# Splitting one exponential in two halves and moving the score rows of 48 turns of an attention kernel

## The chip, the cores and the metric

The kernel runs on one core of one Trainium2 chip. The metric is the device time of one execution in microseconds (us), as a median of runs. Profiles are of one execution each. In the text PE is the matrix engine (its weight loads are listed apart as PEld), ACT the scalar engine, DVE the vector engine, POOL the GpSimd engine, SP the engine that issues most DMAs. SBUF is the on-chip memory that all engines read, PSUM the eight banks into which PE writes its products; a bank holds 512 fp32 numbers in each of 128 partitions.

## The reference, cut to what matters

```python
S, D, H, F = 2048, 512, 32, 1792          # Dh = D // H = 16
xn = layernorm(x)
q, k, v = split(xn @ wqkv)                # 32 heads of 16
p = softmax(einsum("bhqd,bhkd->bhqk", q, k) * Dh ** -0.5)
s = einsum("bhqk,bhkd->bhqd", p, v).reshape(1, S, D) @ wo
h = relu(xn @ w1 + b1) ** 2
g = silu(h @ w2 + b2)
out = x + s * g
```

## The kernel before, in words

A first part normalizes x and makes q, k and v. Then comes a long loop of 64 **turns** (L1142), and a short end. The attention is cut into 1024 steps: 8 groups of four heads, 4 chunks of 512 queries, 16 blocks of 128 keys. A step has two **score pairs** p = 0 and 1, each of two heads hp = 0 and 1. A score (L511) is one multiply of a 64-row half of PE into one bank: 128 keys by 512 queries. The two scores of a pair use the two row halves of PE and run beside each other. The exponential of a score goes into an SBUF tile (ptile) that the values multiply (L863) reads later.

Turn n, with i = 8n, computes the scores of steps i+1 to i+8 and at its end multiplies the values of steps i to i+7. There are 16 score pairs in a turn. Between them PE runs the feed-forward products (gate branch, from layer 1 and 2 blocks) in the same 64-row halves. The order of a turn is written out by hand as a string of **rows**, one letter a row; in a row the two halves of PE run one multiply each, of 512 columns:

- S: both scores of a pair, into one of two **places** of two banks each (tag S, two buffers in turn). ACT takes the exponential of both banks as one 128x1024 operation (L519) into the ptile. That frees the place for the second S row after it.
- L: two products of the feed-forward part (L563), into two banks of a tile called spare (in the profile S<-xh,wf1h and the like; S<-QA,KA is a score).
- 0, 1, a, b, B: **set-aside** scores (L533). The score of one head (or, for B, of both) goes into one of the two set-aside banks, sides[0] (in the profile acc) and sides[1] (lin); DVE copies it at once to the ptile in SBUF (L538), and ACT takes the exponential there, in place, at the end of the turn. 0 is head 0 into acc with an L product in the other half, 1 head 1 into lin, a head 0 into lin, b head 1 into acc.
- / : the swap (L584). POOL writes one note (L588) as soon as the L products so far have ended, and the first L product behind the swap waits for that note, since the two halves of PE change banks.

An ordinary turn has 40 rows. Counted from 0, its S rows are rows 0, 3, 8, 12, 16, 19, 23, 27, 31, 37 and 39, the swap stands between rows 18 and 19, and the set-aside rows are 4 (B), 11 (0), 14 (1), 20 (B), 26 (0), 29 (1), 34 (0) and 36 (1). Nine of the pairs go straight to ACT (pairs 0 to 8), pairs 9 to 13 are set aside, and the last two, both of step i+8, are scored in rows 37 and 39; their exponentials are issued behind those of the set-aside pairs (L1181, L1185), because their ptile is that of step i and comes free only when the values multiply of step i has run. After the rows PE runs the values multiply of eight steps into acc, DVE takes that sum out of acc (L889 or L892), and the next turn begins: a one-element ACT copy and DVE operation (L1129, L1130) first, then row 0.

Row 0 and row 3 of the next turn use the places of the last two pairs, and its row 4 uses acc and lin again.

Of the kernel before, what the change touches and what calls it, by code (L numbers as in the profile page):

```python
# [27 lines left out]
AF = mybir.ActivationFunctionType  # L28
# [7 lines left out]
SCALE = DH ** -0.5  # L36
# [40 lines left out]
def fast_path(tc, sb, banks, env):  # L77
# [7 lines left out]
    dve, act, pool, sp = nc.vector, nc.scalar, nc.gpsimd, nc.sync  # L85
# [6 lines left out]
    def t(shape, dt, tag):  # L92

        cnt[0] += 1
        if tag in BUFS:
            turn[tag] = turn.get(tag, -1) + 1
            n = turn[tag] % BUFS[tag]
            p, tag = ps.get(tag), f"{tag}{places[n] if tag == 'S' else n}"
        else:
            p = None  # L100
        return (p or ps.get(tag, sb)).tile(shape, dt, tag=tag, name=f"{tag}_{cnt[0]}")
# [407 lines left out]
    ptile = {}  # L509

    def score(i, p, hp, dst):  # L511
        qd, qc, kb = steps[i]
        k, q = ka[qd, kb // 8], qa[qd, qc]
        r = slice(64 * hp, 64 * hp + 64)
        mm(dst, k[r, p, 128 * (kb % 8):128 * (kb % 8) + 128], q[r, p], start=True, stop=True)  # L515

    def exps(i, p, src):
        if src is not None:
            act.activation(ptile[i, p], src, AF.Exp, scale=SCALE)  # L519

    def place(i, p):
        ptile[i, p] = t([128, 2, 512], FT, f"P{2 * ((i - 1) % 8) + p}")

    def scores(i, p):

        if i < len(steps):
            sc = t([128, 2, 512], FT, "S")
            place(i, p)
            for hp in range(2):
                score(i, p, hp, sc[:, hp])  # L530
            return sc

    def aside(i, p, hp, bank):  # L533

        if (i, p) not in ptile:
            place(i, p)
        score(i, p, hp, sides[bank])
        dve.tensor_copy(ptile[i, p][:, hp], sides[bank])  # L538
# [37 lines left out]
    def lin(*halves):  # L576
        done = False
        if pair[0]:
            for half in halves:
                j = half ^ swapped[0]  # L580
                done |= pair[0][j].issue(half, lin_banks[j])
        return done

    def swap():  # L584
        if pair[0]:
            while lin(0, 1):
                pass
            f = pool.memset(note[:, notes[0]:notes[0] + 1], 0.0)  # L588
            notes[0] += 1
            for block in pair[0]:  # L590
                tc.add_manual_dep(f.ins, block.last, SYNC, reason="the products so far")
            swapped[0], fence[0] = 1, f.ins.name

    def end_pair():
        if pair[0]:
            while lin(0, 1):
                pass
            swapped[0], last, pair[0] = 0, pair[0], None
            last[0].evict()
# [46 lines left out]
    def second(c, g, i):  # L646
        ms = [m for m in range(len(PAIRS)) if PAIRS[m][0] == g]
        h, w = [hid[m] for m in ms], [wf[2, m] for m in ms]

        def evict():  # L650
            if g == 0:
                y[c, i] = t([128, 2, 512], FT, f"y{i}")
            old = b2b.unsqueeze(1).broadcast_to([128, 2, 512]) if g == 0 else y[c, i]
            dve.tensor_tensor(y[c, i], spare, old, op=OP.add)
            if g == 3:
                complete.add((c, i))

        return [Block(lambda p, k, j=j: h[k // 2][p][:, k % 2, 128 * j:128 * j + 128],
                      lambda p, k: w[k // 2][p][:, k % 2], range(2 * len(ms)), evict)
                for j in (2 * i, 2 * i + 1)]  # L660
# [9 lines left out]
    for c in ORDER:  # L670
        for m in range(len(PAIRS)):
            fill.append([lambda m=m: first(m)])
            if m in (1, 2, 4, 6):
                makes = [lambda c=c, g=m // 2, i=i: second(c, g, i) for i in range(2)]
# [164 lines left out]
    def early():  # L839
        open_banks(below, "ps2", "left", (("S0", 1024), ("S1", 1024)))  # L840
        for q in range(2):
            exps(0, q, scores(0, q))
# [28 lines left out]
    def values_of(steps_now):  # L871
        for i in steps_now:
            values(i, i == steps_now[0], i == steps_now[-1])

    def finish_early():
        early[0] = t([128, 512], FT, "ou")
        dve.tensor_copy(early[0], sides[0])
# [114 lines left out]
    def make_last():  # L992
        u = pend.pop((2, 3))
        h, l = onorm[2, 3] = on_tiles(2, 3)
        o = t([128, 512], FT, "T")
        for a in (h, o):
            pool.tensor_tensor(a, u[:, 0], u[:, 1], op=OP.mult)
        pool.tensor_tensor(l, o, h.bitcast(FT), op=OP.subtract)
# [40 lines left out]
    middle = {}  # L1039
    TURNS, LAST = len(steps) // 8, 8 * (NQ - 1)  # L1040
# [8 lines left out]
    for j, c in enumerate(ORDER):  # L1049
        for i in range(2):  # L1050
            n = per * (j + 1) + i - 1 if j < 3 else LAST + 2 + i
# [41 lines left out]
    def happen(time):  # L1093
        for fn, a in events.pop(int(2 * time), ()):
            fn(*a)
# [6 lines left out]
    sides = [t([128, 512], FT, "acc"), t([128, 512], FT, "lin")]  # L1102
    xs[0] = xT[3]

    def rest(i, dst):

        group(dst, lambda p: onorm[2, 3][p][:, cut[i]], lambda p: wos[0][p][1][:, 1])
# [18 lines left out]
    def see(i):  # L1126

        last = ptile[i, 1][:1, 1, 511:]
        act.copy(seen[:, :1], last)  # L1129
        dve.tensor_tensor(seen[:, 8:9], last, sides[1][:1, :1], op=OP.max)  # L1130
# [1 line left out]

    ASIDES = {"0": ((0, 0),), "1": ((1, 1),), "a": ((0, 1),), "b": ((1, 0),), "B": ((0, 0), (1, 1))}
    ORDINARY = "SLLSBLLLSLL0SL1LSLL/SBLLSLL0SL1LSLL0L1SLS"
    TWO_PAIRS = "SLLSbLaLLS/0SaLLLbS1LSEVSLLSLLLLBS/LLLL0LS1S"

    SHORT = "SLLSBLLLS0S1LL0S1/S0LL1SL0SL1L0LSS1"

    FIRST = "SLLSLLBLSLL0SL1LSLL/SBLLSLL0SL1LSLL0L1SLS"
    for n in range(TURNS):  # L1142
        i = 8 * n
        happen(n)
        makes = fill[n][:]
        pair[0] = makes.pop(0)()
        if n:
            see(i - 1)
        pairs = [(k, p) for k in range(i + 1, i + 9) for p in range(2)]
        short = n in (LAST, LAST + 1)  # L1150
        nd = 8 if short else 9
        direct, asides = pairs[:nd] + pairs[14:], pairs[nd:14]
        later, aside_at = [], [0, 0]
        for row in TWO_PAIRS if makes else SHORT if short else ORDINARY if n else FIRST:
            if row == "S":
                k, p = direct.pop(0)
                sc = scores(k, p)
                if k == i + 8:
                    later.append((k, p, sc))
                else:  # L1160
                    exps(k, p, sc)
            elif row == "L":
                lin(0, 1)
            elif row in ASIDES:
                for hp, bank in ASIDES[row]:
                    aside(*asides[aside_at[hp]], hp, bank)
                    aside_at[hp] += 1
                if len(ASIDES[row]) == 1:
                    lin(1 - hp)
            elif row == "/":  # L1170
                swap()
                if n == TURNS - 1:
                    make_last()
            elif row == "E":
                end_pair()
                pair[0] = makes.pop(0)()
            else:
                values_of(range(i, i + 2))
                finish_early()
        for j, (k, p) in enumerate(asides):  # L1180
            exps(k, p, ptile[k, p])  # L1181
            if j == 0:
                for fn, a in middle.pop(n, ()):
                    fn(*a)
        for a in later:  # L1185
            exps(*a)
        if n == TURNS - 1:
            two = t([128, 2, 512], FT, "S")
            for m in range(2):
                rest(m, two[:, m])  # L1190
            rest(3, sides[1])
        pieces_now = pieces_of[n] if n < len(pieces_of) else 0
        ahead = pieces_now > 0 and n % per in (0, 1, 3, 6, 7, 10, 11)
        while lin(0, 1):
            pass
        if ahead:
            split_piece()
        end_pair()
        if n == LAST + 4:
            gsb.update({(1, i): y[1, i] for i in range(2)})  # L1200
        if n == TURNS - 1:
            for m in range(2):
                end_rest(m, two[:, m])
            end_rest(3, sides[1])
        happen(n + 0.5)
        for _ in range(pieces_now - ahead):
            split_piece()
        values_of(range(i + 2 if early[0] else i, i + 8))
        finish(n)
# [27 lines left out]
    for n in range(2):  # L1237
        for i in range(2):
            for j in range(4):
                k = 8 * n + 4 * i + j  # L1240
# [137 lines left out]
```

## Time and profile before

| what | us |
|---|---|
| median of 3 runs (1207.81 to 1208.74) | 1208.66 |
| the profiled execution's own time | 1208.63 |
| its span, first to last instruction | 1206.9 |
| stretch ahead of the turns' first values multiply | 0 to 145.8 |
| stretch of the turns' values multiplies | 145.8 to 1192.8 |
| the end | 1192.8 to 1206.9 |
| DVE busy in the span | 844.3 |
| ACT busy in the span | 1042.2 |
| POOL busy in the span | 357.1 |

The span is 1.7 us shorter than the profiled execution's time. The trace's granted clock of PE is 0.999 over the span. A line of the timeline has the start in us from the span's start, the duration, the engine, the line of the kernel, the operation, the tiles written and read, shapes and the count, and in brackets how long the engine sat idle before and what ended that. Where operations of one kind overlap, they are merged in one line with a count, and the duration is that of the whole. A PEld line is the load of the weights for a multiply that comes later. Ends of multiplies are modelled, so starts are what is compared.

### The profile page before, as it was taken

To read this page: it belongs to the slowest core of one execution; us is meant where nothing else is said; L and a number is where in the kernel's file an instruction comes from. 1 tells how busy PE (TensorE), PEld (TensorE's weight loads), DVE (VectorE), ACT (ScalarE), POOL (GpSimd) and SP (SyncE) were. 2 spreads that over 40 slices of the span, in tenths; PEclk is the share of its full clock that TensorE was granted. 3 is DMA by queue.
4 is the path that set the end of the run, shared out by engine and by line. 5 is a ranking of instruction groups with operands and counts; after the bars stand their busy time and mean duration, and the time that the engine had idled before them with its cause. 6 is when DMAs were issued, how large, how long until landed. Compare 5 with 4: busy or idle time off the path is not lost.

```text
span 1206.9 us, 24222 instructions
## 1 busy us (share of the span) xinstructions
PE 1197.8 (99%) x9867; PEld 712.8 (59%) x9867; DVE 844.3 (70%) x1362; ACT 1042.2 (86%) x1232; POOL 357.1 (30%) x276
## 2 busy tenths in 40 slices
PE   9999999999999999999999999999999999999997
PEld 7888655555655555655555555555555555555554
DVE  7666767575867776757677666667775758777766
ACT  6655689889989889988999899889898889999984
POOL 6756523040312321304032122220230403322224
PEclk9999999999999999999999999999999999999999
DMA  7798914131343222224423133151422233455434
GB/s 291 297 377 312 339 56 137 45 111 44 97 155 108 72 72 84 68 77 150 119 76 102 58 93 90 45 168 45 132 80 80 78 100 80 132 189 171 159 110 141
DMA packets 107640, 155.17 MB, mean 129 GB/s; under 512 B 43386, under 2 KB 57736, under 8 KB 107524
## 3 DMA queue, kind: packets, MB, share of 16 engines
q1 hardware_dynamic: 104596, 144.60, 37.1%
q0 software_dynamic: 2352, 7.93, 2.1%
q8 instruction: 78, 1.28, 0.5%
q10 hardware_dynamic: 576, 1.05, 0.2%
q14 instruction: 38, 0.31, 0.1%
HBM read 103.87 MB, written 49.67 MB: 127 GB/s over the span
## 4 chain that ended last, share of the span: by engine, by line
PE 98%; DVE 1%; DMA 0%; issue 0%; ACT 0%; DVEq 0%
PE acc L866 37%; PE S L563 29%; PE S L515 15%; PE B L326 5%; PE acc L515 5%; PE B L127 4%; PE lin L515 2%; PE D L326 1%; PE D L253 1%; PE S L1017 0%; PE lin L326 0%; PE acc L326 0%; DMA P<-in_A_x_dram 0%; DVE P L1262 0%; DVE P L1263 0%; PE S L326 0%
## 5 line engine op out<-in xcount | busy, mean ns | idle before, releaser
L519 ACT ACTIVATE P<-S 128x1024 f32<-128x1024 f32 x702 | 662.7, 1039 | 91.8 <-PE S L515 89.0
L866 PE MATMUL acc<-P,V 128*32 128x512 f32 x4096 | 453.5, 594 | 0.0
L538 DVE COPY P<-acc 128x512 f32<-128x512 f32 x322 | 222.8, 692 | 141.5 <-PE acc L515 70.0
L519 ACT ACTIVATE P<-P 128x1024 f32<-128x1024 f32 x322 | 315.0, 1090 | 0.0
L515 PE MATMUL S<-QA,KA 64*128 64x512 f32 x1404 | 295.4, 404 | 0.0
L866 PEld LDWEIGHTS acc<-P,V 128*32 128x32 f32 x4096 | 126.2, 110 | 286.2 <-issue 265.0
L538 DVE COPY P<-lin 128x512 f32<-128x512 f32 x322 | 220.7, 685 | 1.8 <-PE lin L515 0.6
L515 PEld LDWEIGHTS S<-QA,KA 64*128 64x128 f32 x1404 | 136.4, 184 | 109.3 <-issue 41.8
L515 PE MATMUL lin<-QA,KA 64*128 64x512 f32 x322 | 126.4, 393 | 0.0
L515 PE MATMUL acc<-QA,KA 64*128 64x512 f32 x322 | 126.4, 393 | 0.0
L120 POOL TENSOR_TENSOR wf1l<-wr,wf1h 128x1024 fp32r<-128x1024 f32 x28 | 68.4, 2443 | 178.8 <-DVE wf1h L116 110.4
L588 POOL MEMSET note<- 1x1 f32 x68 | 6.0, 88 | 378.8 <-PE S L563 374.4
L563 PE MATMUL S<-xl,wf1h 64*128 64x512 f32 x464 | 95.9, 390 | 0.0
L120 POOL TENSOR_TENSOR hl<-T,hh 128x1024 fp32r<-128x1024 f32 x28 | 80.0, 2857 | 52.9 <-DVE hh L116 52.9
L120 POOL TENSOR_TENSOR wf2l<-wr,wf2h 128x1024 fp32r<-128x1024 f32 x28 | 67.2, 2400 | 90.6 <-DVE wf2h L116 90.6
L563 PE MATMUL S<-wf2l,hh 64*128 64x512 f32 x448 | 91.2, 390 | 0.0
L563 PE MATMUL S<-xh,wf1l 64*128 64x512 f32 x480 | 91.1, 388 | 0.0
L892 DVE TENSOR_TENSOR ou<-acc,ou 128x512 f32<-128x512 f32 x31 | 21.4, 692 | 96.1 <-PE acc L866 90.3
L563 PE MATMUL S<-wf2h,hl 64*128 64x512 f32 x448 | 85.2, 388 | 0.0
L563 PE MATMUL S<-xh,wf1h 64*128 64x512 f32 x480 | 77.7, 391 | 0.0
L563 PE MATMUL S<-wf2h,hh 64*128 64x512 f32 x448 | 72.6, 392 | 0.0
L515 PEld LDWEIGHTS acc<-QA,KA 64*128 64x128 f32 x322 | 59.3, 184 | 15.9 <-DVE P L538 1.9
(379 smaller groups left out, 1434.8 us busy)
## 6 DMA issues: line engine op xcount, KB each, us to landing
wr<-in_B_w_dram SPq DMA_DIRECT2D x56, 512.0 KB
QA<-qd SPq DMA_DIRECT2D x128, 128.0 KB
KA<-kd SPq DMA_DIRECT2D x64, 256.0 KB
u<-ud SPq DMA_DIRECT2D x15, 512.0 KB
kd<-P SPq DMA_DIRECT2D x11, 512.0 KB
V<-vd SPq DMA_DIRECT2D x8, 664.0 KB
qd<-P SPq DMA_DIRECT2D x9, 512.0 KB
vd<-P SPq DMA_DIRECT2D x16, 280.0 KB
```

The lines of the kernel that those rows point to most:

```text
L120: leng.tensor_tensor(lo, src, hi.bitcast(FT), op=OP.subtract)
L127: mm(dst, lhs(a, k), rhs(b, k), start=n == 0, stop=n == len(todo) - 1)
L253: nc.tensor.transpose(halves[k // 2][:, k % 2, 128 * j:128 * j + 128], xnorm[c, i][:, j, 128 * k:128 * k + 128], ident)
L326: mm(dst, left[a][:, k], right[b][:, k], start=n == 0, stop=n == 5)
L515: mm(dst, k[r, p, 128 * (kb % 8):128 * (kb % 8) + 128], q[r, p], start=True, stop=True)
L519: act.activation(ptile[i, p], src, AF.Exp, scale=SCALE)
L538: dve.tensor_copy(ptile[i, p][:, hp], sides[bank])
L563: ins = mm(bank, self.lhs(a, k)[r], self.rhs(b, k)[r], start=n == 0 and self.at[other] == 0, stop=n == len(self.todo[half]) - 1 and self.a ...
L588: f = pool.memset(note[:, notes[0]:notes[0] + 1], 0.0)
L866: mm(sides[0][32 * j:32 * j + 32], vq[qd][:, kb, 17 * j:17 * j + 32], ptile[i, j // 2][:, j % 2], start=first, stop=last)
L892: dve.tensor_tensor(ou, sides[0], part[0], op=OP.add)
```

## The change

In 48 of the 64 turns another string of rows is used (SPREAD). These are all turns but the first and the last, the four that hold two feed-forward pairs, the eight that start a gate (an additional ACT operation), and the two short ones. It still has 40 rows with the same numbers of S, L and set-aside scores. Its S rows are 0, 3, 8, 12, 16, 20, 24, 29, 33 and 38, its set-aside rows 4 (B), 10 (0), 13 (1), 19 (C), 25 (a), 28 (0), 32 (1) and 35 (b), and row 39 is a new kind, Z. C is B with the lin bank first.

The ninth straight pair (row 33) gets two exponentials of 128x512, one for each bank of its place. Row 39 takes no place of its own: head 0 goes into the first bank of row 33's place, once the first half's exponential has read it, and head 1 into lin. So the turn uses ten places and not eleven. Behind the set-aside pairs ACT now first takes the two halves of row 39's pair, then the pair of row 38; before, it was pair 0 of step i+8 first and pair 1 second.

```diff
+    def exps_half(i, p, hp, src):
+        act.activation(ptile[i, p][:, hp], src, AF.Exp, scale=SCALE)
...
-    ASIDES = {"0": ((0, 0),), "1": ((1, 1),), "a": ((0, 1),), "b": ((1, 0),), "B": ((0, 0), (1, 1))}
+    ASIDES = {"0": ((0, 0),), "1": ((1, 1),), "a": ((0, 1),), "b": ((1, 0),), "B": ((0, 0), (1, 1)),
+              "C": ((1, 1), (0, 0))}
     ORDINARY = "SLLSBLLLSLL0SL1LSLL/SBLLSLL0SL1LSLL0L1SLS"
...
+    SPREAD = "SLLSBLLLSL0LS1LLSLL/CSLLLSaLL0SLL1SLbLLSZ"
...
+        spread = 0 < n < TURNS - 1 and n not in middle and not short and not makes
...
+                elif spread and (k, p) == pairs[nd - 1]:
+                    ends = sc[:, 0], sides[1]
+                    for hp in range(2):
+                        exps_half(k, p, hp, sc[:, hp])
...
+            elif row == "Z":
+                k, p = direct.pop(0)
+                place(k, p)
+                for hp in range(2):
+                    score(k, p, hp, ends[hp])
...
+        if spread:
+            for hp in range(2):
+                exps_half(i + 8, 1, hp, ends[hp])
         for a in later:
             exps(*a)
```

More of the change, by code (lines that the diff above doesn't have):

```diff
@@ L1152, in fast_path @@
         direct, asides = pairs[:nd] + pairs[14:], pairs[nd:14]
+        spread = 0 < n < TURNS - 1 and n not in middle and not short and not makes
         later, aside_at = [], [0, 0]
-        for row in TWO_PAIRS if makes else SHORT if short else ORDINARY if n else FIRST:
+        for row in TWO_PAIRS if makes else SHORT if short else SPREAD if spread else ORDINARY if n else FIRST:
             if row == "S":
```

## The prediction

> **What bounds the kernel now.** I read the page first (busy times, then the chain), then the waits, then the timeline of one of the 48 turns, which runs from 747.42 to 763.87.
>
> ```profile
> PE 1197.8 (99%) x9867; PEld 712.8 (59%) x9867; DVE 844.3 (70%) x1362; ACT 1042.2 (86%) x1232; POOL 357.1 (30%) x276
> ...
> PE 98%; DVE 1%; DMA 0%; issue 0%; ACT 0%; DVEq 0%
> ...
> L519 ACT ACTIVATE P<-S 128x1024 f32<-128x1024 f32 x702 | 662.7, 1039 | 91.8 <-PE S L515 89.0
> ```
>
> The chain that ended last is PE for 98%. ACT idles 89.0 us in all, waiting for scores. So PE's issue of rows bounds the turns, and the change leaves PE's rows alone in number and kind. It can gain only where PE waits.
>
> ```profile
> PEld S L515 <- ACT P L519: 22.1, 94, 0.8
> PEld acc L866 <- DVE P L538: 20.0, 66, 0.4
> PEld S L563 <- POOL note L588: 2.9, 18, 0.2
> ```
>
> Those are all of PE's waits of the kinds that the change touches: weight loads (PEld) that wait for an exponential to free a place, for the last DVE copy out of acc, and for POOL's note. They are waits of loads, which go ahead of their multiplies, so they are no loss yet. What is lost is seen in the starts of the rows:
>
> ```profile
> 750.29 0.39 PE L515 MATMUL S<-QA,KA 64*128 64x512 f32 x2
> ...
> 751.20 0.39 PE L515 MATMUL S<-QA,KA 64*128 64x512 f32 x2
> 751.43 0.62 PE L563 MATMUL S<-wf2h,hl 64*128 64x512 f32 x4
> ```
>
> Here nothing waits: from row 12 (750.29) to row 17 (751.43) five rows take 1.14, **0.228 a row**. Around the swap it is otherwise:
>
> ```profile
> 751.81 0.19 PEld L515 LDWEIGHTS S<-QA,KA 64*128 64x128 f32 x2 [0.19 <-ACT P L519]
> 751.88 0.44 PE L515 MATMUL S<-QA,KA 64*128 64x512 f32 x2
> ...
> 752.11 0.09 POOL L588 MEMSET note<- 1x1 f32 x1 [6.54 <-PE S L563]
> 752.15 0.40 PE L515 MATMUL acc<-QA,KA 64*128 64x512 f32 x1
> 752.16 0.40 PE L515 MATMUL lin<-QA,KA 64*128 64x512 f32 x1
> 752.25 0.33 PEld L563 LDWEIGHTS S<-wf2h,hh 64*128 64x128 f32 x4
> 752.38 0.64 PE L563 MATMUL S<-wf2h,hh 64*128 64x512 f32 x4
> 752.58 0.69 DVE L538 COPY P<-acc 128x512 f32<-128x512 f32 x1 [0.72 <-PE lin L515]
> 752.73 0.19 PEld L515 LDWEIGHTS S<-QA,KA 64*128 64x128 f32 x2
> 752.85 0.41 PE L515 MATMUL S<-QA,KA 64*128 64x512 f32 x2
> ```
>
> Row 19's load waits for ACT and starts at 751.81, 0.16 behind where a load goes out with row 18 (751.65, half of the doubled line at 751.43). Row 19 itself is on time (751.88), but row 20 begins 0.27 later: about 0.04 is lost. I read from it that a load is good for its second next row start 0.34 later (751.81 to 752.15), so a load may be about 0.11 late for nothing (2 x 0.228 - 0.34). From row 17 to row 23 six rows take 1.42 instead of 1.37: **0.05 lost**.
>
> ```profile
> 754.36 1.98 ACT L519 ACTIVATE P<-S 128x1024 f32<-128x1024 f32 x2
> ...
> 755.40 0.39 PE L515 MATMUL acc<-QA,KA 64*128 64x512 f32 x1
> ...
> 755.90 0.69 DVE L538 COPY P<-acc 128x512 f32<-128x512 f32 x1 [0.53 <-PE acc L515]
> 756.08 0.39 PE L515 MATMUL S<-QA,KA 64*128 64x512 f32 x2
> 756.17 1.11 ACT L519 ACTIVATE P<-P 128x1024 f32<-128x1024 f32 x1
> 756.31 0.39 PE L563 MATMUL S<-wf2h,hl 64*128 64x512 f32 x2
> 756.40 0.19 PEld L515 LDWEIGHTS S<-QA,KA 64*128 64x128 f32 x2
> ...
> 756.53 0.40 PE L515 MATMUL S<-QA,KA 64*128 64x512 f32 x2
> 756.86 0.16 PEld L866 LDWEIGHTS acc<-P,V 128*32 128x32 f32 x8 [0.28 <-DVE P L538]
> ```
>
> From row 23 (752.85) to row 39 (756.53) 16 rows take 3.68, 0.230 a row, 0.03 above 16 x 0.228. Row 39's load (756.40) is 0.09 behind row 38: it waits for the ninth exponential, which ends at 754.36 + 1.98 = 756.34, and just costs nothing. The values multiply begins at 756.86, 0.33 behind row 39. So the whole of what PE loses in the second half of a turn is about 0.05 + 0.03, and the change can win no more than that: 48 x 0.08 = 3.8 us.
>
> **The change part by part.**
>
> *Score rows a row later.* Row 19's score becomes row 20: its load goes out with row 19, 0.23 later, and the place is free by then (751.81 is 0.07 earlier). The same holds for rows 24, 29 and 33, in place of 23, 27 and 31. All the waits for ACT between rows 19 and 33 go. What is late next is **POOL's note**. It starts when row 18's products end and is there at 752.25, 0.60 behind row 18's start. The first L row stays row 21. Its load used to be 0.10 late (752.25 against row 20's 752.15); with row 20 on time (751.65 + 2 x 0.228 = 752.11) it is 0.14 late, over the 0.11 that costs nothing. Row 22 can start at 752.25 + 0.34 = 752.59 and row 23 at 752.82 instead of 752.85. So 0.03 of the 0.05 is won and 0.02 stays with the note.
>
> *Rows 23 to 39.* No load waits any more; 0.03 above the bare pace is lost now. How much of it comes from waits I bound by nothing (rows 1 to 16, 747.76 to 751.20, run at 0.229 without such waits) and 0.03 (all). I take 0.02, toward the middle.
>
> ```profile
> 747.42 0.50 PE L515 MATMUL S<-QA,KA 64*128 64x512 f32 x2
> 747.76 0.63 PE L563 MATMUL S<-wf2h,hh 64*128 64x512 f32 x4
> 748.23 0.40 PE L515 MATMUL S<-QA,KA 64*128 64x512 f32 x2
> 748.46 0.39 PE L515 MATMUL acc<-QA,KA 64*128 64x512 f32 x1
> ...
> 748.89 0.69 DVE L538 COPY P<-acc 128x512 f32<-128x512 f32 x1 [0.58 <-PE lin L515]
> 749.50 0.68 DVE L538 COPY P<-lin 128x512 f32<-128x512 f32 x1
> ```
>
> *Set-aside rows.* A bank is free again 1.18 behind its row: the copy of acc starts 0.43 after row 4 and takes 0.69 (748.46, 748.89 to 749.58), and a semaphore's 0.06 follows (as 756.34 to 756.40 above). B's second copy ends at 750.18, 1.72 behind the row. A load six rows on goes out at 5 x 0.228 = 1.14, 0.04 late, under the 0.11. Row 10 (acc, six behind row 4), row 25 (lin, six behind C, whose first copy is lin's) and the rest (seven to nine rows) cost nothing. Five rows would have cost 0.16 (1.18 - 4 x 0.228 - 0.11).
>
> *The last copy out of acc* moves from row 34 to row 35 (b). Before, it ended at 755.90 + 0.69 = 756.59, 0.27 ahead of the values multiply. One row (0.23) later leaves 0.04, against a semaphore's 0.06; but row 34's copy began 0.50 behind its row (755.40 to 755.90) where row 4's took 0.43. With 0.43 there is 0.05 to spare. Bounds: 0 to 0.02 lost. I take 0.
>
> *Row 39 (Z).* It needs the first half exponential of row 33's pair, and lin's copy from row 32 (1.18 behind, six rows before: free).
>
> ```profile
> L114 ACT COPY P<-B 128x512 f32<-128x512 f32 x14 | 8.1, 585 | 6.8 <-PE B L127 6.6 <-DMA vd<-P 0.2
> ```
>
> The trace has no half exponential; the nearest row is a 128x512 ACT copy out of PSUM, 585 ns. ACT starts 0.04 behind the end of a row (row 0: 747.42 + 0.50, ACT at 747.96 below), so 0.43 behind row 33, and the half is done and seen at 0.43 + 0.59 + 0.06 = 1.08; Z's load goes out five rows on, at 1.14. Nothing is lost; if it took as long as a whole one (1.04) it would be 0.39 late and cost 0.28, and behind it on PE stands the values multiply, with all that follows. The DVE operation that reads lin at the turn's start (L1130) has row 39's product ready seven microseconds ahead. The change moves no DMA and nothing on POOL's or SP's queue.
>
> *ACT.* Two pairs are now two operations each. Two halves cost at most 2 x 0.585 against 1.039, 0.13 a pair more, and at least nothing. Row 33 stands at 752.82 + 10 x 0.229 = 755.11 and its exponential at 755.54, where the ninth began at about 756.34 - 1.04 = 755.30: 0.24 later. ACT so ends its turn 0.2 to 0.5 later.
>
> ```profile
> 747.96 8.39 ACT L519 ACTIVATE P<-S 128x1024 f32<-128x1024 f32 x9 [1.49 <-PE S L515]
> 756.17 4.88 ACT L519 ACTIVATE P<-P 128x1024 f32<-128x1024 f32 x5
> 760.90 1.97 ACT L519 ACTIVATE P<-S 128x1024 f32<-128x1024 f32 x2
> 762.71 0.17 ACT L1129 COPY seen<-P 1x1 f32<-1x1 f32 x1
> ```
>
> Its cover is the idle time ahead of the next turn's first exponential, 1.49, and the 1.0 from 762.87 to the next row 0 (763.87): it hides all of that. The last set-aside exponential ends at 761.05, at most 761.55 after the change; the step that reads it is the last of eight in the values multiply (7.01 from 756.86, so about 763.0). Without that cover each 0.1 would cost 4.8 us. The Trainium skill (ScalarE: Activation LUTs, What ACT_TABLE_LOAD costs) speaks against the split: an ACTIVATE costs 186 ns beside its 0.833 ns an element, and two in a row overlap by some 93. This case's 1039 agrees with it at 1024 elements. By it, an estimate, each split pair costs ACT 93 ns more, which the idle time hides all the same.
>
> *Sum.* 0.03 + 0.02 = 0.05 a turn, 48 turns: 2.4 us off. The profiled execution's 1208.63 (span 1206.9 and 1.7 around it, both kept) becomes **1206.2**. That execution is within 0.03 of the median 1208.66.
>
> **The rivals.**
>
> *Larger gain.* POOL's note doesn't hold the row, and all waits' after-effects go: 0.05 + 0.03 and some of the 0.33 ahead of the values multiply, 0.08 to 0.1 a turn, about **1204.2**. For it: in the whole span the profile shows only 18 waits for the note. Against: the note's time is fixed by row 18's end.
>
> *No change to speak of.* The note takes back all that ACT's wait gave, as where it comes 0.03 later than here, and rows 23 to 39 keep their pace: 0 to 0.02 a turn, about **1208.0**. That is also the case in which the edit does what it says and only exchanges the waits. A page of the Trainium skill gives it another way (TensorE: Matmul & The Clock Gate, The cost: per-tile semaphore tail): each signal at a multiply's end adds about 26 ns, and rows 33 and 39 now must signal for each bank; by an estimate 2 x 0.026 x 48 = 2.5 us, the gain. As a mechanism of this kernel: were the two rows that signal twice to hold up the next by 0.025 each, the 0.05 would be gone, 1208.6. Row 20 signals for acc and for lin (752.15, 752.16), and row 21 follows at the common 0.23 (752.38), so I give it 0.03 of this rival's chance.
>
> *Slower.* Row 39 can't start on the first half alone: it waits for both, because the half is slower than the copy or because its wait covers the place as a whole. The second half ends about 0.43 + 2 x 0.52 + 0.06 = 1.53 behind row 33 (0.52 is half of 1.04), so Z's load is 0.39 late, 0.28 over the free 0.11: 48 x 0.28 = 13.4, **1217.2** with the gain taken off (2.4). It decides from 1.25 behind row 33 on. Against it: half 0 is the first of ACT's two, and its bank is one of its own. A milder form is the last copy out of acc holding the values multiply by some 0.1: +4.8 - 2.4, 1211.0.
>
> **How the numbers follow.** 0.2% is 2.4 us, about what a measurement of this kernel can tell from no change, so the forecast stands just on that line. Chances: forecast 0.42 (its own range 1204.9 to 1207.4, from 0.03 to 0.08 a turn; 0.24 of it beyond the line), larger gain 0.18, no change 0.24, slower 0.16 (0.10 the dear form, 0.06 the mild one, half of it within the line). Faster: 0.18 + 0.24 = 0.42; same: 0.18 + 0.24 + 0.03 = 0.45; slower 0.13. The range leaves out the dear form of slower, half of the mild one and the outermost of the gain: 1203.4 to 1210.0.
>
> **What the profile will show.** Right: no PEld wait for ACT at rows 20 to 33; the load behind the note about 0.14 late and row 23 at 1.39 behind row 17 (1.42 before); row 39 0.23 behind row 38; ACT's idle time ahead of a turn's first exponential down by 0.2 to 0.5 from 1.49, with another gap of about 0.2 ahead of row 33's; values multiply 0.33 behind row 39. Wrong: a PEld wait at row 39 that ends with the second half exponential, a wait of the values multiply that ends with the copy of row 35, row 25 late behind lin's copy, or the idle time of ACT gone.

## The result: 48 turns each 0.28 us longer

| kernel | median us | lowest to highest | ratio to before, 95% interval |
|---|---|---|---|
| before | 1208.7 | 1207.81 to 1208.92 | 1 |
| changed | 1222.2 | 1221.69 to 1222.83 | 1.0114 [1.0102, 1.0127] |

The changed kernel is 13.5 us slower: 0.28 us for each of the 48 turns. The profiled execution took 1221.69, with a span of 1219.9.

The page of the changed kernel, in the lines that answer to those shown of before (busy times, the chain by engine, the new half exponentials):

```profile
PE 1208.1 (99%) x9867; PEld 719.1 (59%) x9867; DVE 848.6 (70%) x1362; ACT 1057.1 (87%) x1328; POOL 357.3 (29%) x276
...
PE 91%; ACT 7%; DVE 1%; issue 0%; DMA 0%; DVEq 0%
...
L522 ACT ACTIVATE P<-S 128x512 f32<-128x512 f32 x144 | 80.5, 596 | 0.0
```

PE has as many multiplies as before, and ACT has 96 operations more, two a turn. What is new is ACT in the chain, 7% where it had none. The waits of the changed kernel (engine, line, whom it waited for: us in total, times, longest) name the place:

```profile
PEld S L515 <- ACT P L522: 22.8, 48, 0.5
PEld acc L869 <- ACT P L522: 14.4, 48, 0.3
...
PEld S L515 <- ACT P L519: 10.8, 30, 0.8
PEld S L566 <- POOL note L591: 10.3, 58, 0.2
```

Before, PE's loads waited 94 times for whole exponentials; 30 of those are left, none of them at rows 20 to 33 of the 48 turns, so the later score rows did what they were to do. In their stead stand 48 waits of 0.48 on average for a half exponential, one a turn, and POOL's note is now waited for 58 times, not 18. The second line is no new loss: within the values multiply the loads pause 0.30 again and again, in both kernels, nearly always marked "issue" (886 such waits before, 885 now), and once a turn the half exponential is named for it. The end of the same turn as in the prediction, in the timeline of the changed kernel:

```profile
763.39 0.39 PE L515 MATMUL S<-QA,KA 64*128 64x512 f32 x2
...
763.84 1.08 ACT L522 ACTIVATE P<-S 128x512 f32<-128x512 f32 x2
763.84 0.39 PE L515 MATMUL acc<-QA,KA 64*128 64x512 f32 x1
...
764.26 0.69 DVE L541 COPY P<-acc 128x512 f32<-128x512 f32 x1
764.30 0.19 PEld L515 LDWEIGHTS S<-QA,KA 64*128 64x128 f32 x2
764.52 0.95 PE L515 MATMUL S<-QA,KA 64*128 64x512 f32 x3
764.79 1.07 ACT L519 ACTIVATE P<-P 128x1024 f32<-128x1024 f32 x1
...
764.97 0.18 PEld L515 LDWEIGHTS S<-QA,KA 64*128 64x128 f32 x1 [0.48 <-ACT P L522]
764.97 0.18 PEld L515 LDWEIGHTS lin<-QA,KA 64*128 64x128 f32 x1
764.97 0.50 PE L515 MATMUL lin<-QA,KA 64*128 64x512 f32 x1
765.40 0.16 PEld L869 LDWEIGHTS acc<-P,V 128*32 128x32 f32 x8 [0.24 <-issue]
```

Row 33 starts at 763.39. The two half exponentials run from 763.84 to 764.92. Row 39's load goes out at 764.97, 0.05 behind the end of the **second** half, though its head 0 writes only the bank that the first half had read, by about 764.44 (763.84 + 0.60). Row 38 stands at 764.52 (the line of three multiplies is its two and row 39's first), so the load is 0.45 late, row 39 stands at 764.97, 0.45 behind row 38 and not 0.23, and the values multiply follows 0.43 behind that and not 0.33. That is 0.22 + 0.10 = 0.32 a turn, less what the rest of the turn won. (Means over the 48 turns, here and below, are of the profiled execution; a row starts with the earlier of its two multiplies. In that mean row 39 is 0.447 behind row 38 and the values multiply 0.431 behind row 39.)

In the compiled program the first half raises no semaphore, the second raises it by two, and row 39's head 0 waits for the second count. The place is one tile of two banks, and the wait takes in the last reader of the tile, although that one reads the other bank.

### The profile page after: what moved, and what is told of

The parts are those of the page before. It is cut to its first block, busy times and chain, and to the rows that moved or that the text cites. A ratio compares the mean times of both kernels' runs of the same rounds, so it can differ in the third digit from the quotient of the medians.

```text
span 1219.9 us, 24385 instructions
## 1 busy us (share of the span) xinstructions
PE 1208.1 (99%) x9867; PEld 719.1 (59%) x9867; DVE 848.6 (70%) x1362; ACT 1057.1 (87%) x1328; POOL 357.3 (29%) x276
## 4 chain that ended last, share of the span: by engine, by line
PE 91%; ACT 7%; DVE 1%; issue 0%; DMA 0%; DVEq 0%
PE acc L869 37%; PE S L566 23%; PE S L515 14%; PE B L326 5%; PE acc L515 4%; ACT P L519 4%; PE B L127 4%; ACT P L522 4%; PE lin L515 2%; PE D L326 1%; PE D L253 1%; PE S L1020 0%; PE lin L326 0%; DMA P<-in_A_x_dram 0%; PE acc L326 0%
## 5 line engine op out<-in xcount | busy, mean ns | idle before, releaser
L519 ACT ACTIVATE P<-S 128x1024 f32<-128x1024 f32 x606 | 581.2, 1029 | 90.4 <-PE S L515 81.8
L515 PE MATMUL lin<-QA,KA 64*128 64x512 f32 x370 | 150.4, 407 | 0.0
L566 PE MATMUL S<-xh,wf1l 64*128 64x512 f32 x480 | 86.3, 388 | 0.0
L566 PE MATMUL S<-xh,wf1h 64*128 64x512 f32 x480 | 84.8, 393 | 0.0
L522 ACT ACTIVATE P<-S 128x512 f32<-128x512 f32 x144 | 80.5, 596 | 0.0
L566 PE MATMUL S<-wf2h,hl 64*128 64x512 f32 x448 | 80.0, 388 | 0.0
L566 PE MATMUL S<-wf2h,hh 64*128 64x512 f32 x448 | 77.8, 394 | 0.0
```

The costliest lines, as they stand in the source:

```text
L522: act.activation(ptile[i, p][:, hp], src, AF.Exp, scale=SCALE)
L566: ins = mm(bank, self.lhs(a, k)[r], self.rhs(b, k)[r], start=n == 0 and self.at[other] == 0, stop=n == len(self.todo[half]) - 1 and self.a ...
```

## The experiments

**Theory A**: row 39's wait for both halves is the loss. **Theory B**: the last copy out of acc, moved to row 35, holds the values multiply. **Theory C**: the two operations more on ACT, or the place of the ninth pair, cost it.

### Row 39 waits for the first half alone

```diff
     def exps_half(i, p, hp, src):
-        act.activation(ptile[i, p][:, hp], src, AF.Exp, scale=SCALE)
+        return act.activation(ptile[i, p][:, hp], src, AF.Exp, scale=SCALE)
...
-                    for hp in range(2):
-                        exps_half(k, p, hp, sc[:, hp])
+                    halves = [exps_half(k, p, hp, sc[:, hp]) for hp in range(2)]
...
                 for hp in range(2):
-                    score(k, p, hp, ends[hp])
+                    ins = score(k, p, hp, ends[hp])
+                    if hp == 0:
+                        tc.declare_no_dep(ins.ins, halves[1].ins, reason="the second half reads the other bank")
+                        tc.add_manual_dep(ins.ins, halves[0].ins.name, SYNC, reason="the first half has read this bank")
```

score returns its multiply. The two lines replace the wait for the second half, whose bank head 0 doesn't touch, by a wait for the first, whose bank it writes: in this compiled program the first half raises the semaphore itself, and head 0 waits for that count.

> The changed kernel, but row 39's head 0 waits for the end of the first half exponential, whose bank it writes, and no longer for that of the second half, which reads the other bank. Theory A, row 39's wait for both halves is the whole loss: row 39 comes 0.23 behind row 38 (0.45 after the change) and the values multiply 0.33 to 0.34 behind it (0.43), 0.31 a turn less, 48 x 0.31 = 15 us off 1222.2: 1206 to 1208.5. Theory B, the late copy out of acc (row 35) holds the values multiply: row 39 0.23 behind row 38, but the multiply still 0.43 behind row 39: about 1211.5. Theory C, the two operations more on ACT or the place of the ninth pair cost it: over 1215.

Measured: **1207.45** (1206.22 to 1207.87, 11 runs), ratio 0.9989 [0.998, 0.9998] to before's 1208.65 on the same chip. That is theory A, 14.8 us from one wait. Its timeline in the same turn:

```profile
754.11 0.40 PE L515 MATMUL S<-QA,KA 64*128 64x512 f32 x2
...
754.56 1.08 ACT L522 ACTIVATE P<-S 128x512 f32<-128x512 f32 x2
...
754.98 0.69 DVE L541 COPY P<-acc 128x512 f32<-128x512 f32 x1
755.01 0.19 PEld L515 LDWEIGHTS S<-QA,KA 64*128 64x128 f32 x2
755.24 0.40 PE L515 MATMUL S<-QA,KA 64*128 64x512 f32 x2
755.24 0.18 PEld L515 LDWEIGHTS lin<-QA,KA 64*128 64x128 f32 x1
755.25 0.18 PEld L515 LDWEIGHTS S<-QA,KA 64*128 64x128 f32 x1
755.47 0.39 PE L515 MATMUL lin<-QA,KA 64*128 64x512 f32 x1
755.48 0.39 PE L515 MATMUL S<-QA,KA 64*128 64x512 f32 x1
...
755.79 0.16 PEld L869 LDWEIGHTS acc<-P,V 128*32 128x32 f32 x8 [0.35 <-DVE P L541]
```

Row 39's loads go out with row 38 (755.24), without a wait, and row 39 follows at 0.23 (755.47). The halves are the same (1.08 for both), and the second ends at 755.64, 0.17 behind row 39's start: no harm, as it reads another bank. The values multiply stands 0.32 behind row 39. The copy out of acc ends at 755.67, 0.12 ahead of it. The bracket names that copy, as it did before the change, when it had ended 0.27 ahead; over the 48 turns the load goes out 0.11 behind the copy's end, and where a load does wait for such a copy (the ninth pair a row earlier, below) it is 0.05. So theory B falls here; theory C falls with the time.

### The rows alone, and the rows with the split

```diff
-    SPREAD = "SLLSBLLLSL0LS1LLSLL/CSLLLSaLL0SLL1SLbLLSZ"
+    SPREAD = "SLLSBLLLSL0LS1LLSLL/CSLLLSaLL0SLL1SLbLLSS"
...
-                elif spread and (k, p) == pairs[nd - 1]:
+                elif False:
...
-        if spread:
-            for hp in range(2):
-                exps_half(i + 8, 1, hp, ends[hp])
```

> The new order of rows alone: row 39 is a plain S row in a place of its own turn, all exponentials whole, eleven places a turn, exponentials of the last step in the old order. Theory A: row 39 needs the whole ninth exponential, which starts 0.45 behind row 33, takes 1.03, and is seen 0.05 later: 1.53 behind row 33, against a load due at 1.14, so 0.39 late, about 0.28 lost, 0.03 won elsewhere: 48 x 0.25 = 12 us over before, 1219 to 1222. Theory C, the split is what costs: 1207 to 1209.

Measured: **1218.9**, ratio 1.0084 [1.0069, 1.01], 0.1 under the range that was expected for theory A and far from theory C's. A plain row 39, which needs the whole ninth exponential, is nearly as late as the changed kernel's: 0.393 behind row 38 in the mean of the 48 turns (0.447 there), with the values multiply 0.430 behind it.

The second kernel has the same string and drops the same last three lines, but keeps the split of the ninth pair (the elif stays as in the changed kernel):

> As the new order of rows alone, but the ninth pair's exponential in two halves; row 39 is still a plain S row, writes both banks of row 33's place and nothing of lin. Theory A: it waits for the second half as the changed kernel does, 1.58 behind row 33: within 1.5 us of the changed kernel, 1221 to 1224, and 1 to 3 us over the rows alone, which is the split's own price. Were row 39's use of lin what costs, it would be well under 1219.

Measured: **1222.25**, ratio 1.0111 [1.0096, 1.0127]: the changed kernel's time. Row 39's half place and lin gave nothing at all; with its wait on the second half the row is as late as a plain row would be. The split's own price, 1222.25 - 1218.9, is 3.35 us or 0.07 a turn, 0.35 us over the 1 to 3 that were expected; in these two kernels row 39 hangs on its end.

### Rows 19 and 20 exchanged

```diff
+    EXCHANGED = "SLLSBLLLSLL0SL1LSLL/BSLLSLL0SL1LSLL0L1SLS"
...
-        for row in TWO_PAIRS if makes else SHORT if short else ORDINARY if n else FIRST:
+        for row in TWO_PAIRS if makes else SHORT if short else EXCHANGED if spread else ORDINARY if n else FIRST:
```

(spread is the same 48 turns; the rest is the kernel before.)

> The kernel before, with rows 19 and 20 alone exchanged in the 48 turns (the set-aside row first, the score after it). If the score's wait for ACT at row 19 was the loss around the swap and POOL's note takes a part of it back: the load behind the note 0.15 late, 0.02 to 0.03 a turn won, 1207 to 1208. If the note holds nothing: 0.05 to 0.08 a turn, 1204.8 to 1206.3. If the exchange brings a new wait: 1209 or more.

Measured: **1213.67**, ratio 1.0041 [1.0027, 1.0055]. The edit brought the new wait of the last case: it puts B at row 19, five rows behind the use of lin at row 14, where before there were six. The timeline of this kernel:

```profile
754.19 0.39 PE L515 MATMUL lin<-QA,KA 64*128 64x512 f32 x1
754.61 0.69 DVE L538 COPY P<-lin 128x512 f32<-128x512 f32 x1
755.08 0.18 PEld L515 LDWEIGHTS acc<-QA,KA 64*128 64x128 f32 x1
755.30 0.39 PE L515 MATMUL acc<-QA,KA 64*128 64x512 f32 x1
755.36 0.18 PEld L515 LDWEIGHTS lin<-QA,KA 64*128 64x128 f32 x1
755.36 0.50 PE L515 MATMUL lin<-QA,KA 64*128 64x512 f32 x1
```

Row 14 uses lin at 754.19, its copy ends at 755.30, and the load into lin for row 19 goes out 0.06 later (755.36), 0.28 behind the row's other load (755.08). The loss isn't paid there: the half of PE with the late multiply falls behind the other one. In the 48 turns the two multiplies of row 19 start 0.07 apart (median), those of row 20 0.17 and those of row 27 still 0.10; at row 28 they are together again, and rows 23 to 33 take 2.440 in the mean, 2.316 before. The next kernel mends that distance, by moving the set-aside rows 11 and 14 to rows 10 and 13:

```diff
-    EXCHANGED = "SLLSBLLLSLL0SL1LSLL/BSLLSLL0SL1LSLL0L1SLS"
+    EXCHANGED = "SLLSBLLLSL0LS1LLSLL/BSLLSLL0SL1LSLL0L1SLS"
```

> The kernel before with rows 19 and 20 exchanged and, in the first half, the set-aside rows at 10 and 13 as in the changed kernel, so that no use of acc or lin follows the last by fewer than six rows (five in the exchange alone: row 14 to row 19, lin). If that one distance was what made the exchange alone slow: lin is waited for no more, 5 us come back, and the row order wins 0 to 0.04 a turn (row 20's score free of ACT, POOL's note late 0.15, rows 23 and 27 on their old edge): 1206.7 to 1208.8. If the exchange has another cost: 1211 or more.

Measured: **1208.51**, ratio 1.0 [0.9991, 1.0009]. The 5 us are gone, and rows 23 to 33 are back at 2.315, so one row too few between two uses of lin costs 0.11 a turn by the times and 0.125 in that stretch. This edit does two things, though, and they cancel: by the means over the 48 turns the exchange wins 0.014 from row 17 to row 23 (1.414, before 1.428), and the turn loses 0.015 from row 0 to row 17 (4.022; 4.007 both before and in the exchange alone), where rows 10 and 13 are new. The waits show ACT's hardly fewer and the note's new:

```profile
PEld S L515 <- ACT P L519: 20.3, 90, 0.8
...
PEld S L563 <- POOL note L588: 10.3, 58, 0.2
```

Row 19's 48 waits for ACT are gone from the 48 turns, but rows 23 and 27 now have 62, where before row 23 alone had 19, and the note is waited for in every one of these turns, before in 9.

### The ninth pair a row earlier

Whole exponentials first, as in the rows alone. The eighth pair goes a row earlier too, with the set-aside rows beside them a row later, and row 38's score goes to row 37:

```diff
-    SPREAD = "SLLSBLLLSL0LS1LLSLL/CSLLLSaLL0SLL1SLbLLSS"
+    SPREAD = "SLLSBLLLSL0LS1LLSLL/CSLLLSaLLS0LLS1LbLSLS"
```

> The rows alone, whole exponentials, eleven places, but the eighth and ninth straight pairs a row earlier (28 and 32, not 29 and 33), and row 38's score at row 37. By the rule of the late load: the ninth exponential is seen 1.53 behind row 32, row 39's load due at 6 x 0.228 = 1.37, 0.16 late, 0.05 lost against 0.28: about 48 x 0.21 = 10 us under the rows alone (1218.9): 1208 to 1210.5. If the place in the order isn't what decides, it stays over 1215.

Measured: **1210.56**, ratio 1.0017 [1.0007, 1.0026]; 8.3 us under the rows alone (before's median beside it was 1208.39), 0.06 over the top of what was expected. So the distance between the ninth pair and row 39 decides most of it: row 39's load goes out 0.15 behind row 38 in the mean of the 48 turns, and row 39 still follows at 0.230. The 0.05 that was expected to stay does, but not there. The end of a turn:

```profile
757.74 0.68 DVE L541 COPY P<-acc 128x512 f32<-128x512 f32 x1
...
757.98 0.19 PEld L515 LDWEIGHTS S<-QA,KA 64*128 64x128 f32 x2 [0.18 <-ACT P L519]
758.04 0.44 PE L515 MATMUL S<-QA,KA 64*128 64x512 f32 x2
...
758.47 0.16 PEld L869 LDWEIGHTS acc<-P,V 128*32 128x32 f32 x8 [0.30 <-DVE P L541]
```

The copy out of acc ends at 758.42 and the values multiply's load goes out 0.05 behind it, in all 48 turns; the values multiply stands 0.396 behind row 39 in the mean, before 0.337. Then the same move, of the eighth and ninth pairs alone, in the kernel with the right wait:

```diff
-    SPREAD = "SLLSBLLLSL0LS1LLSLL/CSLLLSaLL0SLL1SLbLLSZ"
+    SPREAD = "SLLSBLLLSL0LS1LLSLL/CSLLLSaLLS0LLS1LbLLSZ"
```

> The kernel whose row 39 waits for the first half alone (1207.45), with the eighth and ninth pairs a row earlier. There no load is late any more except behind POOL's note, so nothing is left to win: within 0.7 us of it, 1206.7 to 1208.2. If row 39's half place was still on the edge, it gets 1 to 3 us faster.

Measured: **1210.87**, ratio 1.002 [1.0011, 1.0029], a miss: 3.4 us slower than the 1207.45 that it should have kept, and over the expected range. The timeline shows why:

```profile
757.30 0.39 PE L515 MATMUL lin<-QA,KA 64*128 64x512 f32 x1
757.61 0.18 PEld L515 LDWEIGHTS acc<-QA,KA 64*128 64x128 f32 x1
757.72 0.69 DVE L541 COPY P<-lin 128x512 f32<-128x512 f32 x1 [0.16 <-PE lin L515]
757.76 0.39 PE L515 MATMUL acc<-QA,KA 64*128 64x512 f32 x1
758.33 0.68 DVE L541 COPY P<-acc 128x512 f32<-128x512 f32 x1
...
758.67 0.39 PE L515 MATMUL lin<-QA,KA 64*128 64x512 f32 x1
...
759.07 0.14 PEld L869 LDWEIGHTS acc<-P,V 128*32 128x32 f32 x5 [0.42 <-DVE P L541]
```

The move put the set-aside rows 33 (lin) and 35 (acc) two rows apart, 0.46. DVE needs 0.61 from one copy to the next (757.72 to 758.33), so the copy out of acc starts 0.57 behind its row and ends at 759.01, and the values multiply's load goes out 0.06 behind that, 0.40 behind row 39 (758.67). This is theory B's mechanism, which the changed kernel does not have; this one has it, and so has the kernel with whole exponentials, whose two rows are the same. In the mean of the 48 turns the values multiply stands 0.395 behind row 39, with the ninth pair at row 33 it is 0.328: 48 x 0.067 = 3.2 of the 3.4 us.

## Why the prediction was wrong

The step that failed is the one on **row 39**: "It needs the first half exponential of row 33's pair" and "Nothing is lost". The row's head 0 needs the first half, but the wait in the program is for the second, since the place is one tile. The prediction had this as its slower rival ("its wait covers the place as a whole"), with a chance of 0.10, and argued against it that the half's bank "is one of its own". That is true of the memory and was no argument about the wait: what mattered was which of the two exponentials signals, and nothing in the trace of before shows a place that is freed by halves. The range's upper end, 1210.0, left the case out. Its first sign of being wrong, "a PEld wait at row 39 that ends with the second half exponential", is the line at 764.97.

That rival's mechanism was right, and its price of 0.28 a turn near: the load came 0.45 late where 0.39 was worked out, since the halves began 0.45 behind row 33 and not 0.43 and took 1.08 together and not 1.04. Row 39 lost 0.22 and the values multiply 0.10, 0.32 together. The time that went with it is not the sum of its terms, however: 1208.6 + 13.4 - 2.4 is 1219.6, and 1217.2 takes the gain off twice. (A smaller slip: 0.03 a turn off 1208.6 is 1207.2, not the 1207.4 of the forecast's own range.) Measured were 1222.2, 2.6 over that sum: 1.9 for the 0.04 a turn, and the rest because the other rows won less than 2.4.

The other steps, in the changed kernel or in the one with the right wait:

- *Score rows a row later*: right in the waits, too large in the gain. No row from 20 to 33 waits for ACT in any of the 48 turns, and the changed kernel's timeline around the swap shows the note late next:

```profile
760.15 0.40 PE L515 MATMUL acc<-QA,KA 64*128 64x512 f32 x1
...
760.38 0.09 POOL L591 MEMSET note<- 1x1 f32 x1 [7.32 <-PE S L566]
760.39 0.40 PE L515 MATMUL S<-QA,KA 64*128 64x512 f32 x2
760.53 0.53 PEld L566 LDWEIGHTS S<-wf2h,hh 64*128 64x128 f32 x6 [0.18 <-POOL note L591]
```

  Row 20 stands at 760.39 and the load behind the note at 760.53, the forecast 0.14 late. But row 23 comes 1.41 behind row 17 in the mean (1.42 with the right wait), not 1.39; before it was 1.43. Of the 0.03 that were to be won here, 0.011 came.
- *Set-aside rows*: nearly right. In none of the 48 turns is a load listed as waiting for a copy six rows back, but the turns lose 0.014 from row 0 to row 17, where rows 10 and 13 were moved and nothing was to be lost; which of the two moves costs it, and how, no run shows. (Row 19 is six rows behind row 13 in lin, too; the prediction counted it among seven to nine.) The price put on five rows, 0.16, was measured as 0.11 to 0.125.
- *The last copy out of acc*: right for the change (with the right wait it ends 0.12 ahead of the values multiply, which leaves 0.06 beside the semaphore's 0.06; 0.05 forecast), and 0.07 a turn lost as soon as another copy stands two rows ahead of it.
- *ACT*: right in the main. The halves of row 33's pair take 1.08 where a whole one takes 1.03; the rule of the Trainium skill (ScalarE: Activation LUTs, What ACT_TABLE_LOAD costs) gave 0.09 more for a split pair, the trace 0.05. With the right wait the idle time ahead of a turn's first exponential is 1.06 where it was 1.49, 0.43 less, within 0.2 to 0.5:

```profile
763.34 1.03 ACT L519 ACTIVATE P<-S 128x1024 f32<-128x1024 f32 x1 [1.06 <-PE S L515]
```

  The other gap that was forecast, of about 0.2 ahead of row 33's exponential, isn't there: the profile shows no idle time of ACT ahead of any half exponential.
- *Rows 33 and 39 signalling for each bank* (the second ground of the rival with no change): at row 33 this didn't arise. In the compiled program its second multiply alone signals, and row 34 follows at 0.227 in the mean.
- *Sum*: 0.05 a turn, 2.4 us, was forecast for the rest of the change; with the right wait 1.2 us were measured (1208.65 to 1207.45), by the interval 0.2 to 2.4. How it divides, the profiled executions show, in means over the 48 turns (that of the kernel with the right wait, 1206.22, is the fastest of its eleven runs, so its total is on the high side):

| us | rows 0 to 17 | 17 to 23 | 23 to 38 | 38 to 39 | 39 to values multiply | sum |
|---|---|---|---|---|---|---|
| before | 4.007 | 1.428 | 3.458 | 0.230 | 0.337 | 9.460 |
| changed | 4.020 | 1.411 | 3.428 | 0.447 | 0.431 | 9.738 |
| row 39 waits for the first half | 4.021 | 1.417 | 3.424 | 0.227 | 0.328 | 9.418 |

  With the right wait 0.042 a turn are won. That this is near the 0.05 is in part luck: around the swap 0.011 came and not 0.03, rows 23 to 39 gave 0.037 and not 0.02, the values multiply stands 0.009 nearer, and rows 0 to 17 lost 0.014 that no term had.

So the change's idea holds, if by little: the version with the wait on the first half is faster than before by 0.11%, with an interval, [0.02%, 0.2%], that just excludes no change.

## What to carry to other kernels

Here, splitting a read to free half a buffer early gained nothing until the half's own reader signalled and the next writer waited for that signal; look at what the wait is drawn against (here the whole tile) before pricing it by what the memory needs. Where one place is handed on at a fixed distance, count the distance in rows against the time from the row to the free buffer: five rows instead of six cost 5 us, the ninth pair one row nearer to row 39 some 8. And when a row is moved, check the queue of each engine that serves it, not only the one that it was moved for: two copies on DVE two rows apart were some 3 us. An edit that moves several rows can win in one stretch and lose in another; times of stretches show what the total hides.

## What was not expected of the hardware

A set-aside multiply whose bank came late didn't hold the one beside it: in the exchange of rows 19 and 20 the multiply into acc started at 755.30 and the one in the other half of PE, into lin, at 755.36. From there the two halves ran up to 0.21 apart, for some nine rows, where in the kernel before the two multiplies of a row start 0.01 apart in the median and never over 0.06 in these turns. And two half exponentials in a row take 1.08 together, 0.05 over the 1.03 of a whole one, less than the 0.13 that was taken as the bound; between the two kernels with a plain row 39, one with the split, 3.35 us or 0.07 a turn were measured.
